# Exponential chains on VectorE in seven operations instead of eight, and a third tile in the fifth chunk of six batches

## The chip, the cores and the metric

The kernel runs on one core of a Trainium2 chip. The metric is the device time of one execution in microseconds (us). Engines are named as in the profile: PE (TensorE, matrix products), DVE (VectorE), ACT (ScalarE), POOL (GpSimd) and SP (SyncE, which here only issues DMAs).

## The reference

The program is soft-capped attention followed by a soft mixture of experts with 8 experts and 32 slots. Inputs are q, k, v of 8 batches x 12 heads x 448 positions x 64.

```python
scores = scale * np.matmul(q, k.transpose(0, 1, 3, 2))     # scale = 1/8
scores = cap * np.tanh(scores / cap)                       # cap = 30
attn = np.exp(scores - np.max(scores, axis=-1, keepdims=True))
attn = attn / (np.sum(attn, axis=-1, keepdims=True) + 1e-09)
x = np.matmul(attn, v)                                     # then (B*S, H*D) = (3584, 768)
logits = x @ phi
slot_input = softmax(logits, axis=0).T @ x                 # 32 slots
slot_out[e] = np.maximum(slot_input[e] @ w1[e], 0) @ w2[e] # 8 experts of 4 slots
out = softmax(logits, axis=1) @ slot_out
```

The two softmaxes of the last part are written out in the original. What the change touches is the exponential of the capped scores; the kernel takes no maximum away, since scores stay within 30.

## The kernel before

Attention is worked off in tiles. Two heads make a pair, two pairs a quad (Q); each pair has seven tiles of scores, a tile being 128 partitions (64 keys of each of the two heads) by 448 queries. The 48 pairs give 336 tiles. Six tiles make a chunk, so there are 56 chunks, seven to a batch of the input. A chunk is worked in two halves of three tiles.

For each half, PE forms the scores (`qk_chunk`, L320) in one of two PSUM tiles `sc`, and ACT writes tanh of them as float16 into the chunk's tile `ex` (`tanh_chunk`, L329). A PSUM tile is free for the scores two halves on when its tanh is done. Then the exponential is taken in place, float16 to bfloat16. ACT does most tiles (`exp_chunk`, `exp_part`, L334); the first tiles of some chunks are done on DVE by a chain of eight elementwise steps (`poly_exp`, L564 to L572) which builds the bits of the bfloat16 number: the first step scales into 16-bit fixed point, the next takes the fraction (`xf`), the next four form a cubic polynomial of it (`xp`), the seventh adds it and the last scales to the bfloat16 pattern. `SHARED` says how many tiles of a chunk go this way, and `POLY` in which place of DVE's queue each step of each chain is issued. All chains use one `xf` and one `xp`.

PE multiplies the exponentials with the values (`pv_first`, `pv_rest`, L590; block-diagonal values `vbd`, cast by POOL at L287) in one PSUM bank `pv`. DVE normalizes (`norm`: reciprocal L597, product L600) into `xq`. Transposes of q and k (`transp`: PE L277 into `qps`/`kps`, DVE copy L279), of the attention output (`x_transp`: PE L638 and L643 into `xps`, DVE copy L652 to `xT`), the logits, the slot sums (`slacc`, L741) and the transposed slot weights all share one PSUM bank with the tag T: each of them waits until the one before has been copied out.

The order on every engine is written by hand. The loop over chunks j has slots; `at(j, slot, f)` hangs work into a slot, and `run(j, slot)` issues what hangs under "<slot", "slot" and ">slot" in that order:

```python
        run(j, "e")          # after the tanh of both halves of chunk j
        exp_chunk(j - 1)     # from j = 3 on
        pv_first(pr); run(j, "a"); pv_tail(pr, 0, CA)
        qk_chunk(2 * j + 2); run(j, "b")
        pv_rest(pr, aux.pop((j, "r"), ())); vcast_after(pr); run(j, "c")
        qk_chunk(2 * j + 3); run(j, "d")
```

The x transpose of a batch's first quad is in slot "a" of the batch's sixth chunk, and q of the next batch's first quad is transposed in slot "b" of the same chunk. Dummy products (`fill` L620, `spare` L835 and L838) keep PE at work. After the last chunk the expert layers and the output follow; they are not touched.

Of the kernel before, what the change touches and what calls it, by code (L numbers as in the profile page):

```python
# [12 lines left out]
U16 = mybir.dt.uint16  # L13
F16 = mybir.dt.float16
ALU = mybir.AluOpType
# [17 lines left out]
STEP = 512  # L33
POW2 = (0.07802411, 0.2260679, 0.69583317, 0.99992526)
# [3 lines left out]
def kernel(  # L38
# [297 lines left out]
    def exp_chunk(j):  # L336
# [4 lines left out]
    SHARED = {1: (2, 0), 3: (2, 0), 4: (3, 0), 6: (1, 0), 7: (3, 0), 9: (3, 0), 11: (2, 0), 12: (3, 0),  # L341
# [4 lines left out]
    POLY = {(1, 'e'): ((1, 0),),  # L346
            (1, '>b'): ((1, 1), (1, 2)),
            (1, 'r'): ((1, 3),),
            (1, '<c'): ((1, 4),),
            (1, '>c'): ((1, 5),),  # L350
            (2, '>a'): ((1, 6),),
            (2, '>c'): ((1, 7),),
            (3, 'e'): ((3, 0), (3, 1), (3, 2)),
            (3, '>b'): ((3, 3),),
            (4, '>a'): ((3, 4), (3, 5), (3, 6), (4, 0)),
            (4, '<c'): ((4, 1),),
            (5, 'e'): ((3, 7), (4, 2)),
            (5, '>a'): ((4, 3),),
            (6, 'e'): ((4, 4), (4, 5)),
            (6, '>a'): ((6, 0), (4, 6), (6, 1)),  # L360
            (6, '>b'): ((6, 2),),
            (6, 'r'): ((4, 7),),
            (6, '<c'): ((6, 3),),
            (6, '>c'): ((6, 4),),
            (6, '>d'): ((6, 5), (6, 6)),
            (7, 'e'): ((7, 0), (6, 7)),
            (7, '>b'): ((7, 1),),
            (7, '>c'): ((7, 2),),
            (7, '>d'): ((7, 3),),
            (8, 'e'): ((7, 4),),  # L370
            (8, '>a'): ((7, 5),),
            (8, '>c'): ((7, 6),),
            (9, '>a'): ((9, 0), (7, 7)),
            (9, '>b'): ((9, 1),),
            (9, '<c'): ((9, 2),),
            (10, 'e'): ((9, 3),),
            (10, '>a'): ((9, 4),),
            (10, '>b'): ((9, 5),),
            (10, '>c'): ((9, 6),),
            (11, 'e'): ((11, 0), (9, 7), (11, 1)),  # L380
            (11, '>a'): ((11, 2),),
            (11, '<c'): ((11, 3),),
            (11, '>d'): ((11, 4), (11, 5), (11, 6)),
            (12, '>a'): ((11, 7), (12, 0)),
            (12, '>b'): ((12, 1),),
            (12, '<c'): ((12, 2),),
            (12, '>c'): ((12, 3),),
            (13, '>b'): ((12, 4),),
            (13, '>c'): ((12, 5),),
            (13, '>d'): ((12, 6),),  # L390
            (14, 'e'): ((14, 0), (12, 7)),
            (14, '>b'): ((14, 1),),
            (14, '>c'): ((14, 2), (14, 3)),
            (14, '>d'): ((14, 4),),
            (15, '>b'): ((14, 5),),
            (15, '>c'): ((14, 6),),
            (15, '>d'): ((14, 7),),
            (16, '>a'): ((16, 0),),
            (16, '>b'): ((16, 1),),
            (16, '>c'): ((16, 2),),  # L400
            (16, '>d'): ((16, 3),),
            (17, 'e'): ((16, 4),),
            (17, '>a'): ((16, 5),),
            (17, '>d'): ((16, 6),),
            (18, 'e'): ((18, 0), (16, 7)),
            (18, '>a'): ((18, 1), (18, 2)),
            (18, '<c'): ((18, 3),),
            (18, '>d'): ((18, 4), (18, 5)),
            (19, 'e'): ((18, 6),),
            (19, '>a'): ((18, 7), (19, 0)),  # L410
            (19, '>b'): ((19, 1),),
            (19, '<c'): ((19, 2),),
            (20, 'e'): ((19, 3),),
            (20, '>b'): ((19, 4), (19, 5)),
            (20, '>d'): ((19, 6),),
            (21, 'e'): ((21, 0), (19, 7)),
            (21, '>b'): ((21, 1),),
            (21, '>c'): ((21, 2), (21, 3)),
            (21, '>d'): ((21, 4),),
            (22, '>b'): ((21, 5),),  # L420
            (22, '>c'): ((21, 6),),
            (22, '>d'): ((21, 7),),
            (23, '>a'): ((23, 0),),
            (23, '>b'): ((23, 1),),
            (23, '>c'): ((23, 2),),
            (23, '>d'): ((23, 3),),
            (24, 'e'): ((23, 4),),
            (24, '>a'): ((23, 5),),
            (24, '>d'): ((23, 6),),
            (25, 'e'): ((25, 0), (23, 7)),  # L430
            (25, '>a'): ((25, 1), (25, 2)),
            (25, '<c'): ((25, 3),),
            (25, '>d'): ((25, 4), (25, 5)),
            (26, 'e'): ((25, 6),),
            (26, '>a'): ((25, 7), (26, 0)),
            (26, '>b'): ((26, 1),),
            (26, '<c'): ((26, 2),),
            (27, 'e'): ((26, 3),),
            (27, '>b'): ((26, 4), (26, 5)),
            (27, '>d'): ((26, 6),),  # L440
            (28, 'e'): ((28, 0), (26, 7)),
            (28, '>b'): ((28, 1),),
            (28, '>c'): ((28, 2), (28, 3)),
            (28, '>d'): ((28, 4),),
            (29, '>b'): ((28, 5),),
            (29, '>c'): ((28, 6),),
            (29, '>d'): ((28, 7),),
            (30, '>a'): ((30, 0),),
            (30, '>b'): ((30, 1),),
            (30, '>c'): ((30, 2),),  # L450
            (30, '>d'): ((30, 3),),
            (31, 'e'): ((30, 4),),
            (31, '>a'): ((30, 5),),
            (31, '>d'): ((30, 6),),
            (32, 'e'): ((32, 0), (30, 7)),
            (32, '>a'): ((32, 1), (32, 2)),
            (32, '<c'): ((32, 3),),
            (32, '>d'): ((32, 4), (32, 5)),
            (33, 'e'): ((32, 6),),
            (33, '>a'): ((32, 7), (33, 0)),  # L460
            (33, '>b'): ((33, 1),),
            (33, '<c'): ((33, 2),),
            (34, 'e'): ((33, 3),),
            (34, '>b'): ((33, 4), (33, 5)),
            (34, '>d'): ((33, 6),),
            (35, 'e'): ((35, 0), (33, 7)),
            (35, '>b'): ((35, 1),),
            (35, '>c'): ((35, 2), (35, 3)),
            (35, '>d'): ((35, 4),),
            (36, '>b'): ((35, 5),),  # L470
            (36, '>c'): ((35, 6),),
            (36, '>d'): ((35, 7),),
            (37, '>a'): ((37, 0),),
            (37, '>b'): ((37, 1),),
            (37, '>c'): ((37, 2),),
            (37, '>d'): ((37, 3),),
            (38, 'e'): ((37, 4),),
            (38, '>a'): ((37, 5),),
            (38, '>d'): ((37, 6),),
            (39, 'e'): ((39, 0), (37, 7)),  # L480
            (39, '>a'): ((39, 1), (39, 2)),
            (39, '<c'): ((39, 3),),
            (39, '>d'): ((39, 4), (39, 5)),
            (40, 'e'): ((39, 6),),
            (40, '>a'): ((39, 7), (40, 0)),
            (40, '>b'): ((40, 1),),
            (40, '<c'): ((40, 2),),
            (41, 'e'): ((40, 3),),
            (41, '>b'): ((40, 4), (40, 5)),
            (41, '>d'): ((40, 6),),  # L490
            (42, 'e'): ((42, 0), (40, 7)),
            (42, '>b'): ((42, 1),),
            (42, '>c'): ((42, 2), (42, 3)),
            (42, '>d'): ((42, 4),),
            (43, '>b'): ((42, 5),),
            (43, '>c'): ((42, 6),),
            (43, '>d'): ((42, 7),),
            (44, '>a'): ((44, 0),),
            (44, '>b'): ((44, 1),),
            (44, '>c'): ((44, 2),),  # L500
            (44, '>d'): ((44, 3),),
            (45, 'e'): ((44, 4),),
            (45, '>a'): ((44, 5),),
            (45, '>d'): ((44, 6),),
            (46, 'e'): ((46, 0), (44, 7)),
            (46, '>a'): ((46, 1), (46, 2)),
            (46, '<c'): ((46, 3),),
            (46, '>d'): ((46, 4), (46, 5)),
            (47, 'e'): ((46, 6), (47, 0)),
            (47, '>a'): ((46, 7), (47, 1)),  # L510
            (47, '>b'): ((47, 2),),
            (47, '<c'): ((47, 3),),
            (47, '>c'): ((47, 4),),
            (48, 'e'): ((48, 0),),
            (48, '>a'): ((47, 5),),
            (48, 'r'): ((47, 6), (47, 7)),
            (48, '>c'): ((48, 1),),
            (48, '>d'): ((48, 2),),
            (49, '>a'): ((48, 3), (48, 4), (49, 0)),
            (49, '<c'): ((48, 5), (48, 6)),  # L520
            (49, '>c'): ((49, 1),),
            (49, '>d'): ((49, 2), (49, 3)),
            (50, '>b'): ((49, 4),),
            (50, '>c'): ((48, 7), (49, 5)),
            (50, '>d'): ((49, 6),),
            (51, 'e'): ((51, 0), (51, 1)),
            (51, '>a'): ((49, 7), (51, 2)),
            (51, '<c'): ((51, 3),),
            (51, '>d'): ((51, 4), (51, 5)),
            (52, 'e'): ((52, 0),),  # L530
            (52, '>a'): ((51, 6),),
            (52, '>b'): ((52, 1),),
            (52, '<c'): ((52, 2), (51, 7)),
            (52, '>d'): ((52, 3),),
            (53, 'e'): ((52, 4), (52, 5)),
            (53, '>a'): ((53, 0), (52, 6)),
# [654 lines left out]
```

## Time and profile before

| what | value |
| --- | --- |
| time, median of 3 runs | 287.41 us (286.95, 287.41, 288.18) |
| span of the profiled execution, first to last instruction | 285.1 us |
| time of the profiled execution with what lies around the span | not listed apart; the median lies 2.3 us above the span |
| busy: PE, DVE, ACT, POOL | 249.9, 243.6, 254.5, 139.4 us |
| mean granted PE clock | 0.983 |
| instructions of the chains on DVE | 34 chains of 8 |
| tiles on DVE | 82 (18 chains of three, 12 of two, 4 of one) |
| ACT exponentials | 21 of six tiles, 4 of five, 12 of four, 19 of three, and some smaller ones |

In the timelines the columns are start and duration in us, engine, line and operation, tiles and shapes, the count, and in brackets the idle time of the engine before it with what ended it. Operations that stand next to each other and are alike are merged in one row. Busy PE is modelled, since products are pipelined. Waits are put down to whatever came last.

The attention part lasts until about 241 us of the span; in it a batch of seven chunks recurs about every 28.8 us.

### The profile page before, as it was taken

How to read it: one execution, taken by the hardware profiler on the slowest of the kernel's cores; microseconds unless marked ns; L12 is line 12 of the kernel's file. 1: busy time of each engine (PE TensorE's matmuls, PEld its weight loads, DVE VectorE, ACT ScalarE, POOL GpSimd, SP SyncE). 2: the span in 40 equal slices, each digit the busy share in tenths (PEclk: the TensorE clock that was granted, in tenths of full speed). 3: DMA queues.
4: the chain of work that ended last, by engine and by line, in shares of the span. 5: the costliest groups of instructions: out<-in, count | busy, mean ns of one | idle time of the engine just before them, and what ended most of it. 6: DMA issues, size and time to landing. Idle time of an engine off the chain costs nothing.

```text
span 285.1 us, 10742 instructions
## 1 busy us (share of the span) xinstructions
PE 249.9 (88%) x4692; PEld 169.8 (60%) x4692; DVE 243.6 (85%) x507; ACT 254.5 (89%) x211; POOL 139.4 (49%) x197
## 2 busy tenths in 40 slices
PE   8888889998999889989998999899899999998720
PEld 7555466756675667566656676667666668552410
DVE  3498999999999999999999999999999986457840
ACT  4999999999999999999999999999999998237730
POOL 7892645664755565565556646564572220200000
PEclk9999999999999999999999999999999999999985
DMA  7999999999999999999999999999999576989997
GB/s 253 241 199 204 216 191 221 217 207 214 218 228 202 205 230 222 228 198 228 226 220 206 218 228 215 209 228 220 223 175 221 129 258 201 409 320 390 410 426 305
DMA packets 58334, 68.10 MB, mean 239 GB/s; under 512 B 4145, under 2 KB 54449, under 8 KB 58289
## 3 DMA queue, kind: packets, MB, share of 16 engines
q0 software_dynamic: 42448, 35.31, 79.4%
q1 hardware_dynamic: 15552, 31.89, 31.9%
q8 instruction: 36, 0.59, 0.8%
q10 hardware_dynamic: 288, 0.23, 0.2%
q14 instruction: 10, 0.07, 0.1%
HBM read 91.72 MB, written 19.27 MB: 389 GB/s over the span
## 4 chain that ended last, share of the span: by engine, by line
DVE 43%; PE 30%; issue 10%; ACT 6%; POOL 6%; DMA 1%; DVEq 0%; ACTq 0%; SPq 0%
PE pv L590 9%; DVE xq L600 7%; PE sc L320 5%; DVE ex L571 4%; DVE xp L570 4%; DVE xT L652 4%; DVE xp L568 3%; POOL vbd L287 3%; DVE qT L279 3%; DVE ex L564 2%; ACT ex L334 2%; DVE xf L566 2%; PE junk L835 2%; DVE xp L569 2%; PE so_ps L1055 2%
## 5 line engine op out<-in xcount | busy, mean ns | idle before, releaser
L329 ACT ACTIVATE ex<-sc 128x1344 f16<-128x1344 f32 (+1 forms) x113 | 149.8, 1454 | 1.4 <-PE sc L320 1.4
L334 ACT ACTIVATE ex<-ex 128x2688 bf16<-128x2688 f16 (+5 forms) x58 | 116.8, 2027 | 0.1
L590 PE MATMUL pv<-vbd,ex 128*128 128x130 bf16 (+1 forms) x1610 | 95.2, 211 | 11.3 <-POOL vbd L287 8.4
L590 PEld LDWEIGHTS <-ex 128*128 128x128 bf16 (+1 forms) x1680 | 75.7, 101 | 36.0 <-PE sc L320 8.9
L320 PE MATMUL sc<-qT,kT 64*64 64x448 bf16 x672 | 71.5, 360 | 0.6 <-DVE qT L279 0.4
L287 POOL CAST vbd<-vraw 64x896 bf16<-64x896 f32 x46 | 46.3, 1006 | 48.9 <-issue 23.9
L600 DVE TENSOR_TENSOR xq<-pv,rec 128x448 bf16<-128x448 f32 x46 | 28.7, 624 | 1.6
L320 PEld LDWEIGHTS <-kT 64*64 64x64 bf16 x672 | 24.2, 105 | 6.4 <-issue 4.2
L295 POOL MEMSET vbd<- 64x1 bf16 x22 | 3.6, 165 | 45.2 <-PE pv L590 45.2
L570 DVE TENSOR_TENSOR xp<-xp,xf 128x1344 f16<-128x1344 f16 (+2 forms) x34 | 25.1, 737 | 0.8
L571 DVE TENSOR_TENSOR ex<-ex,xp 128x1344 uint16<-128x1344 uint16 (+2 forms) x34 | 25.2, 741 | 0.4
L568 DVE TENSOR_TENSOR xp<-xp,xf 128x1344 f16<-128x1344 f16 (+2 forms) x34 | 24.9, 734 | 0.6
L116 POOL DMA_DIRECT2D w1b<-in_moe_w_dram x32 | 25.3, 793 | 0.0
L567 DVE TENSOR_SCALAR xp<-xf 128x1344 f16<-128x1344 uint16 (+2 forms) x34 | 17.0, 501 | 0.4
L184 POOL DMA_DIRECT2D qb<-in_q_dram x22 | 16.7, 758 | 0.8 <-DMA kraw<-in_k_dram 0.8
L279 DVE COPY kT<-kps 128x896 bf16<-128x896 bf16 x23 | 14.1, 615 | 3.1 <-PE kps L274 2.8
L572 DVE TENSOR_SCALAR ex<-ex 128x1344 uint16<-128x1344 uint16 (+2 forms) x34 | 16.4, 484 | 0.1
L277 PEld LDWEIGHTS <-qb 128*64 128x64 bf16 x308 | 10.1, 109 | 10.8 <-issue 10.8
L184 POOL DMA_DIRECT2D kb<-in_k_dram x22 | 16.2, 734 | 0.0
L120 POOL DMA_DIRECT2D w2d<-in_moe_w_dram x21 | 15.9, 777 | 0.4 <-issue 0.4
L620 PE MATMUL pv<-ones 128*128 128x57 bf16 x369 | 15.8, 188 | 0.0
L652 DVE COPY xT<-xps 128x896 bf16<-128x896 bf16 (+1 forms) x24 | 14.3, 597 | 1.7 <-PE xps L643 1.7
(124 smaller groups left out, 343.0 us busy)
## 6 DMA issues: line engine op xcount, KB each, us to landing
w1b<-in_moe_w_dram POOLq DMA_DIRECT2D x32, 384.0 KB, 8.8
vraw<-in_v_dram SPq DMA_DIRECT2D x44, 224.0 KB, 6.1
w2d<-in_moe_w_dram POOLq DMA_DIRECT2D x21, 384.0 KB, 8.4
w2t<-w2d SPq DMA_DIRECT2D x21, 384.0 KB, 7.0
out_dram<-ob SPq DMA_DIRECT2D x7, 768.0 KB, 7.0
qb<-in_q_dram POOLq DMA_DIRECT2D x22, 224.0 KB, 7.4
kb<-in_k_dram POOLq DMA_DIRECT2D x22, 224.0 KB, 6.1
w2b<-in_moe_w_dram POOLq DMA_DIRECT2D x11, 384.0 KB, 8.6
```

Of the source, the lines that this page charges most:

```text
L116: pool.dma_start(out=w1b[e][:, js, fs], in_=w1r[:, e, js, fs])
L184: pool.dma_start(out=t, in_=quad_ap(nm, Q))
L287: pool.tensor_copy(vbds[Q % 2][r, :, :, c0:c0 + DH], raw[r])
L320: pe.matmul(sc[cs, u, 0:S], qkT["k", Q][r, c, cs], qkT["q", Q][r, :, cs], start=True, stop=True)
L329: act.activation(exs[j][:, half * CS + u0:half * CS + u1, :].bitcast(F16), (own[0] if i == u0 == 0 else sc)[:, u0:u1, 0:S], ACT.Tanh, scal ...
L334: act.activation(exs[j][:, u0:u1, :], exs[j][:, u0:u1, :].bitcast(F16), ACT.Exp, scale=cap)
L568: lambda: dve.tensor_tensor(p, p, f, op=ALU.mult),
L570: lambda: dve.tensor_tensor(p, p, f, op=ALU.mult),
L571: lambda: dve.tensor_tensor(y, y, p, op=ALU.add),
L590: pe.matmul(out_, exs[j][r, u, q0:q0 + (HP if tail else P)], v_, start=(c == 0 and g == gs[0] < NF), stop=(c == NT - 1), skip_group_check= ...
L600: dve.tensor_tensor(xq[Q][:, h, s0:s1, :], pv[:, 0:s1 - s0, 0:DH], rec.to_broadcast([P, s1 - s0, DH]), op=ALU.mult)
L652: copy(xTs[Q][:, hs[0]:hs[-1] + 1, :], ps[:, hs[0]:hs[-1] + 1, :])
```

## The change

A chain on DVE has seven steps instead of eight. The fraction is taken with an OR of 512 added in the same instruction, so that it stands for 1 + fraction; its square is formed by one product of the 16-bit integers with the same bits read as float16; one scale-and-add and one product make the polynomial. The fitted constant is moved from the first step to the last.

In chunks 11, 18, 25, 32, 39 and 46, the fifth of their batches, DVE takes three tiles instead of two, so that ACT's exponential of these chunks covers three instead of four. DVE has 88 tiles in all.

`POLY` is written anew: one step fewer for each chain, the others for the most part in the slots where they were. Chunk 39 stands for the six, and its neighbours 37 and 40 for the other chains:

```diff
-POW2 = (0.07802411, 0.2260679, 0.69583317, 0.99992526)
+POW2 = (0.45804578, 0.46570838, 0.07629315)
...
-    SHARED = {... 37: (3, 0), 39: (2, 0), 40: (3, 0), ...}
+    SHARED = {... 37: (3, 0), 39: (3, 0), 40: (3, 0), ...}
...
             (37, '>a'): ((37, 0),),
             (37, '>b'): ((37, 1),),
-            (37, '>c'): ((37, 2),),
-            (37, '>d'): ((37, 3),),
-            (38, 'e'): ((37, 4),),
-            (38, '>a'): ((37, 5),),
-            (38, '>d'): ((37, 6),),
-            (39, 'e'): ((39, 0), (37, 7)),
-            (39, '>a'): ((39, 1), (39, 2)),
-            (39, '<c'): ((39, 3),),
-            (39, '>d'): ((39, 4), (39, 5)),
-            (40, 'e'): ((39, 6),),
-            (40, '>a'): ((39, 7), (40, 0)),
+            (37, '>d'): ((37, 2),),
+            (38, 'e'): ((37, 3),),
+            (38, '>a'): ((37, 4),),
+            (38, '>d'): ((37, 5),),
+            (39, 'e'): ((39, 0), (37, 6)),
+            (39, '>a'): ((39, 1),),
+            (39, '<c'): ((39, 2),),
+            (39, '>d'): ((39, 3), (39, 4)),
+            (40, 'e'): ((39, 5),),
+            (40, '>a'): ((39, 6), (40, 0)),
             (40, '>b'): ((40, 1),),
-            (40, '<c'): ((40, 2),),
-            (41, 'e'): ((40, 3),),
-            (41, '>b'): ((40, 4), (40, 5)),
-            (41, '>d'): ((40, 6),),
+            (41, 'e'): ((40, 2),),
+            (41, '>b'): ((40, 3), (40, 4)),
+            (41, '>d'): ((40, 5),),
...
-    c3, c2, c1, c0 = (c * STEP ** (1 - n) for c, n in zip(POW2, (3, 2, 1, 0)))
-    c1, c0 = c1 - 1, c0 - STEP
+    c0, c1, c3 = POW2
...
-        y, f, p = t.bitcast(U16), xf[x][:, 0:n1], xp[x][:, 0:n1]
+        y, s, p = t.bitcast(U16), xf[x][:, 0:n1], xp[x][:, 0:n1]
         steps = (
-            lambda: dve.tensor_scalar(y, t.bitcast(F16), octaves * STEP, base * STEP + c0,
+            lambda: dve.tensor_scalar(y, t.bitcast(F16), octaves * STEP, base * STEP,
                                       ALU.mult, ALU.add),
-            lambda: dve.tensor_scalar(f, y, STEP - 1, None, ALU.bitwise_and),
-            lambda: dve.tensor_scalar(p, f, c3, c2, ALU.mult, ALU.add),
-            lambda: dve.tensor_tensor(p, p, f, op=ALU.mult),
-            lambda: dve.tensor_scalar(p, p, c1, None, ALU.add),
-            lambda: dve.tensor_tensor(p, p, f, op=ALU.mult),
+            lambda: dve.tensor_scalar(s, y, STEP - 1, STEP, ALU.bitwise_and, ALU.bitwise_or),
+            lambda: dve.tensor_tensor(p, s, s.bitcast(F16), op=ALU.mult),
+            lambda: dve.tensor_scalar(p, p, c3 * 2 ** 24 / STEP ** 2, c1 - 1, ALU.mult, ALU.add),
+            lambda: dve.tensor_tensor(p, p, s, op=ALU.mult),
             lambda: dve.tensor_tensor(y, y, p, op=ALU.add),
-            lambda: dve.tensor_scalar(y, y, 128.0 / STEP, 128.0 * (127 - base),
+            lambda: dve.tensor_scalar(y, y, 128.0 / STEP, 128.0 * (127 - base + c0),
                                       ALU.mult, ALU.add))
```

More of the change, by code (lines that the diff above doesn't have):

```diff
@@ new lines @@
+            (1, '>b'): ((1, 1),),
+            (1, 'r'): ((1, 2),),
+            (1, '<c'): ((1, 3),),
+            (1, '>c'): ((1, 4),),
+            (2, '>a'): ((1, 5),),
+            (2, '>c'): ((1, 6),),
+            (3, 'e'): ((3, 0), (3, 1)),
+            (3, '>b'): ((3, 2),),
+            (4, '>a'): ((3, 3), (3, 4), (3, 5), (4, 0)),
+            (4, '<c'): ((4, 1),),
+            (5, 'e'): ((3, 6),),
+            (5, '>a'): ((4, 2),),
+            (6, 'e'): ((4, 3), (4, 4)),
+            (6, '>a'): ((6, 0), (4, 5), (6, 1)),
@@ new lines @@
+            (6, 'r'): ((4, 6),),
+            (6, '<c'): ((6, 2),),
+            (6, '>c'): ((6, 3),),
+            (6, '>d'): ((6, 4), (6, 5)),
+            (7, 'e'): ((7, 0), (6, 6)),
+            (7, '>b'): ((7, 1),),
+            (7, '>d'): ((7, 2),),
+            (8, 'e'): ((7, 3),),
+            (8, '>a'): ((7, 4),),
+            (8, '>c'): ((7, 5),),
+            (9, '>a'): ((9, 0), (7, 6)),
+            (9, '>b'): ((9, 1),),
+            (10, 'e'): ((9, 2),),
+            (10, '>a'): ((9, 3),),
@@ new lines @@
+            (10, '>b'): ((9, 4),),
+            (10, '>c'): ((9, 5),),
+            (11, 'e'): ((11, 0), (9, 6), (11, 1)),
+            (11, '<c'): ((11, 2),),
+            (11, '>d'): ((11, 3), (11, 4), (11, 5)),
+            (12, '>a'): ((11, 6), (12, 0)),
+            (12, '>b'): ((12, 1),),
+            (12, '>c'): ((12, 2),),
+            (13, '>b'): ((12, 3),),
+            (13, '>c'): ((12, 4),),
+            (13, '>d'): ((12, 5),),
+            (14, 'e'): ((14, 0), (12, 6)),
+            (14, '>b'): ((14, 1),),
@@ L398 @@
+            (14, '>c'): ((14, 2),),
+            (14, '>d'): ((14, 3),),
+            (15, '>b'): ((14, 4),),
+            (15, '>c'): ((14, 5),),
+            (15, '>d'): ((14, 6),),
             (16, '>a'): ((16, 0),),
             (16, '>b'): ((16, 1),),
[L400 to L406, printed above, removed]
@@ L420 @@
-            (22, '>b'): ((21, 5),),
-            (22, '>c'): ((21, 6),),
-            (22, '>d'): ((21, 7),),
+            (16, '>d'): ((16, 2),),
+            (17, 'e'): ((16, 3),),
+            (17, '>a'): ((16, 4),),
+            (17, '>d'): ((16, 5),),
+            (18, 'e'): ((18, 0), (16, 6)),
+            (18, '>a'): ((18, 1),),
+            (18, '<c'): ((18, 2),),
+            (18, '>d'): ((18, 3), (18, 4)),
+            (19, 'e'): ((18, 5),),
+            (19, '>a'): ((18, 6), (19, 0)),
@@ L423 @@
+            (19, '>b'): ((19, 1),),
+            (20, 'e'): ((19, 2),),
+            (20, '>b'): ((19, 3), (19, 4)),
+            (20, '>d'): ((19, 5),),
+            (21, 'e'): ((21, 0), (19, 6)),
+            (21, '>b'): ((21, 1),),
+            (21, '>c'): ((21, 2),),
+            (21, '>d'): ((21, 3),),
+            (22, '>b'): ((21, 4),),
+            (22, '>c'): ((21, 5),),
+            (22, '>d'): ((21, 6),),
             (23, '>a'): ((23, 0),),
             (23, '>b'): ((23, 1),),
-            (23, '>c'): ((23, 2),),
@@ L439 @@
-            (27, '>b'): ((26, 4), (26, 5)),
-            (27, '>d'): ((26, 6),),
-            (28, 'e'): ((28, 0), (26, 7)),
-            (28, '>b'): ((28, 1),),
[L443 to L447, printed above, removed]
+            (23, '>d'): ((23, 2),),
+            (24, 'e'): ((23, 3),),
+            (24, '>a'): ((23, 4),),
+            (24, '>d'): ((23, 5),),
@@ new lines @@
+            (25, 'e'): ((25, 0), (23, 6)),
+            (25, '>a'): ((25, 1),),
+            (25, '<c'): ((25, 2),),
+            (25, '>d'): ((25, 3), (25, 4)),
+            (26, 'e'): ((25, 5),),
+            (26, '>a'): ((25, 6), (26, 0)),
+            (26, '>b'): ((26, 1),),
+            (27, 'e'): ((26, 2),),
+            (27, '>b'): ((26, 3), (26, 4)),
+            (27, '>d'): ((26, 5),),
+            (28, 'e'): ((28, 0), (26, 6)),
+            (28, '>b'): ((28, 1),),
+            (28, '>c'): ((28, 2),),
@@ L448 @@
+            (28, '>d'): ((28, 3),),
+            (29, '>b'): ((28, 4),),
+            (29, '>c'): ((28, 5),),
+            (29, '>d'): ((28, 6),),
             (30, '>a'): ((30, 0),),
             (30, '>b'): ((30, 1),),
[L450 to L457, printed above, removed]
@@ L471 @@
-            (36, '>c'): ((35, 6),),
-            (36, '>d'): ((35, 7),),
+            (30, '>d'): ((30, 2),),
+            (31, 'e'): ((30, 3),),
+            (31, '>a'): ((30, 4),),
+            (31, '>d'): ((30, 5),),
+            (32, 'e'): ((32, 0), (30, 6)),
+            (32, '>a'): ((32, 1),),
+            (32, '<c'): ((32, 2),),
+            (32, '>d'): ((32, 3), (32, 4)),
+            (33, 'e'): ((32, 5),),
+            (33, '>a'): ((32, 6), (33, 0)),
+            (33, '>b'): ((33, 1),),
@@ L473 @@
+            (34, 'e'): ((33, 2),),
+            (34, '>b'): ((33, 3), (33, 4)),
+            (34, '>d'): ((33, 5),),
+            (35, 'e'): ((35, 0), (33, 6)),
+            (35, '>b'): ((35, 1),),
+            (35, '>c'): ((35, 2),),
+            (35, '>d'): ((35, 3),),
+            (36, '>b'): ((35, 4),),
+            (36, '>c'): ((35, 5),),
+            (36, '>d'): ((35, 6),),
             (37, '>a'): ((37, 0),),
             (37, '>b'): ((37, 1),),
-            (37, '>c'): ((37, 2),),
-            (37, '>d'): ((37, 3),),
@@ L498 @@
+            (43, '>b'): ((42, 4),),
+            (43, '>c'): ((42, 5),),
+            (43, '>d'): ((42, 6),),
             (44, '>a'): ((44, 0),),
             (44, '>b'): ((44, 1),),
[L500 to L513, printed above, removed]
+            (44, '>d'): ((44, 2),),
+            (45, 'e'): ((44, 3),),
+            (45, '>a'): ((44, 4),),
+            (45, '>d'): ((44, 5),),
+            (46, 'e'): ((46, 0), (44, 6)),
+            (46, '>a'): ((46, 1),),
+            (46, '<c'): ((46, 2),),
+            (46, '>d'): ((46, 3), (46, 4)),
@@ L514 @@
+            (47, 'e'): ((46, 5), (47, 0)),
+            (47, '>a'): ((46, 6), (47, 1)),
+            (47, '<c'): ((47, 2),),
+            (47, '>c'): ((47, 3),),
             (48, 'e'): ((48, 0),),
-            (48, '>a'): ((47, 5),),
-            (48, 'r'): ((47, 6), (47, 7)),
+            (48, '>a'): ((47, 4),),
+            (48, 'r'): ((47, 5), (47, 6)),
             (48, '>c'): ((48, 1),),
-            (48, '>d'): ((48, 2),),
-            (49, '>a'): ((48, 3), (48, 4), (49, 0)),
-            (49, '<c'): ((48, 5), (48, 6)),
+            (49, '>a'): ((48, 2), (48, 3), (49, 0)),
@@ L521 @@
+            (49, '<c'): ((48, 4), (48, 5)),
             (49, '>c'): ((49, 1),),
[L522 to L525, printed above, removed]
+            (49, '>d'): ((49, 2),),
+            (50, '>b'): ((49, 3),),
+            (50, '>c'): ((48, 6), (49, 4)),
+            (50, '>d'): ((49, 5),),
             (51, 'e'): ((51, 0), (51, 1)),
-            (51, '>a'): ((49, 7), (51, 2)),
-            (51, '<c'): ((51, 3),),
@@ L538 @@
-            (53, '<c'): ((53, 2), (53, 3)),
-            (54, 'e'): ((53, 4),),
-            (54, '>b'): ((53, 5), (53, 6)),
+            (52, '<c'): ((51, 6),),
+            (52, '>d'): ((52, 2),),
+            (53, 'e'): ((52, 3), (52, 4)),
+            (53, '>a'): ((53, 0), (52, 5)),
+            (53, '>b'): ((52, 6), (53, 1)),
+            (53, '<c'): ((53, 2),),
+            (54, 'e'): ((53, 3),),
+            (54, '>b'): ((53, 4), (53, 5)),
             (54, '<c'): ((54, 0),),
-            (54, '>c'): ((53, 7), (54, 1), (54, 2), (54, 3)),
```

107 lines of the change are left out of this document (11 added, 96 removed), and 6 rows, old and new, of the table SHARED.

## The prediction

> **What bounds the kernel now.** I read the page's first part, then the busy times in stretches of one batch, then the timelines of ACT, DVE and PE over one batch, and last the list of waits.
>
> ```profile
> PE 249.9 (88%) x4692; PEld 169.8 (60%) x4692; DVE 243.6 (85%) x507; ACT 254.5 (89%) x211; POOL 139.4 (49%) x197
> ```
> ```profile
> 151.10:179.80 28.70, 26.72 (x553) 18.80 (x551) 27.93 (x57) 28.70 (x23) 17.40 (x25) 1.00 1.25 218
> ```
> The second is one batch; its columns are length, then PE, weight loads, DVE, ACT, POOL busy, then clock, DMA share and GB/s. ACT is busy for all of it, DVE for 97%, PE for 93%, at a full granted clock. The timeline of ACT says the same:
>
> ```profile
> 31.76 1.29 ACT L329 ACTIVATE ex<-sc 128x1344 f16<-128x1344 f32 x1 [0.34 <-PE sc L320]
> 140.47 2.63 ACT L334 ACTIVATE ex<-ex 128x2688 bf16<-128x2688 f16 x1
> 169.24 2.76 ACT L334 ACTIVATE ex<-ex 128x2688 bf16<-128x2688 f16 x1
> ...
> 173.91 2.04 ACT L334 ACTIVATE ex<-ex 128x1792 bf16<-128x1792 f16 x1
> 175.50 2.81 ACT L329 ACTIVATE ex<-sc 128x1344 f16<-128x1344 f32 x2
> ```
> The same exponential of three batches ends at 143.10, 172.00 and, with a start of 198.00 and 2.90, at 200.90: 28.90 apart both times. So ACT sets the pace. But durations of one shape creep up while starts run ahead, so a start is not when work began, and ACT's spare time must be read from ends. Where a tanh truly waited for PE (31.76, ending 33.05), its scores had ended at 31.72 (PE's L320 from 31.15, 0.57): end of scores to end of tanh takes at least 1.33. The spare time of any tanh is that distance less 1.33.
>
> The tightest place comes once a batch: the second tanh of the pair at 175.50, ending 178.31, in the seventh stage. Its scores are the last line here (PE, then DVE ahead of it):
>
> ```profile
> 173.67 0.25 PE L643 MATMUL xps<-ident,xq 64*64 64x64 bf16 x4
> ...
> 174.74 0.58 PE L277 MATMUL qps<-ident,qb 128*64 128x128 bf16 x14 [0.32 <-DVE xT L652]
> 175.25 0.90 PE L590 MATMUL pv<-vbd,ex 128*128 128x130 bf16 x15
> 176.04 0.57 PE L320 MATMUL sc<-qT,kT 64*64 64x448 bf16 x6
> ```
> ```profile
> 170.78 0.21 DVE L597 RECIPROCAL rec<-pv 128x7 f32<-128x7 f32 x1
> 171.02 0.62 DVE L600 TENSOR_TENSOR xq<-pv,rec 128x448 bf16<-128x448 f32 x1
> 171.56 0.68 DVE L568 TENSOR_TENSOR xp<-xp,xf 128x896 f16<-128x896 f16 x1
> 172.16 0.38 DVE L741 TENSOR_TENSOR slacc<-slps,slacc 128x224 f32<-128x224 f32 x1
> 172.46 0.38 DVE L569 TENSOR_SCALAR xp<-xp 128x896 f16<-128x896 f16 x1
> 172.87 0.62 DVE L570 TENSOR_TENSOR xp<-xp,xf 128x896 f16<-128x896 f16 x1
> 173.53 0.62 DVE L571 TENSOR_TENSOR ex<-ex,xp 128x896 uint16<-128x896 uint16 x1
> 174.07 0.61 DVE L652 COPY xT<-xps 128x896 bf16<-128x896 bf16 x1
> ```
> The spare time there is 178.31 - 176.60 - 1.33 = 0.38. Read likewise (0.01 apart by rounding) it is 0.05, 0.40, 0.09, 0.24, 0.37 and 0.13 in the six batches, 1.28 in sum. DVE is why: after the norm (L600) it runs four steps of the fifth chunk's chain, here the two-tile one, and only then copies xT. PE has turned xps by 173.92, the copy starts at 174.07, and PE's qps waits for it because both use the one psT bank. The sixth batch shows what more steps do:
>
> ```profile
> 202.91 0.39 DVE L564 TENSOR_SCALAR ex<-ex 128x896 uint16<-128x896 f16 x1
> 203.21 0.62 DVE L652 COPY xT<-xps 128x896 bf16<-128x896 bf16 x1
> ```
> ```profile
> 203.88 0.58 PE L277 MATMUL qps<-ident,qb 128*64 128x128 bf16 x14 [0.64 <-DVE xT L652]
> ```
>
> **The change, part by part.** *ACT.* In six batches the fifth chunk's exponential covers three tiles instead of four: rows 173.91 to 175.50 (1.59) against 177.84 to 179.05 (1.21), 0.38 each, 2.3 us in all. This is the whole possible gain, as ACT has no other work less.
>
> *DVE's total.* By the groups kept apart by shape, a three-tile chain costs 534+501+610+854+506+855+864+579 = 5303 ns, a two-tile one 4041. The new chain drops one TENSOR_SCALAR (L567, 610). Its and/or step is nearest to L566 (501), its s*s to L568 (854, which already mixes f16 with 16-bit integers), the next to L569 (506): 5303-610 = 4693. A batch goes from 3x5303+4041 = 19950 to 4x4693 = 18772 ns, 1.18 less, so DVE as a total is no bound. The two new kinds are not in the trace. From below I take the shortest three-tile row, 0.50; from above the slope of the f32 rows L741 (224 elements, 381 ns) and L600 (448, 624), which gives 1.60 for 1344 elements. I take the near rows, same size and type width; the upper end is a rival.
>
> *Order on DVE, on the path.* What counts is start to start. With three tiles a TENSOR_TENSOR takes 0.77 to a next step that doesn't need it (150.69 to the copy at 151.47) and 0.89 to one that does (155.86 to 156.76); a TENSOR_SCALAR 0.42 and 0.53 (150.16 to 150.69). Between norm and xT copy the new program issues s*s, slacc, scale-and-add, product and sum of three tiles. Norm to copy was 0.54+0.60+0.30+0.41+0.66+0.54 = 3.05; it becomes 0.54+0.77+0.30+0.53+0.89+0.77 = 3.80. The dropped step lies ahead of the norm, whose start waits for PE, so it gives nothing here. The copy comes 0.75 later, and with it qps, the 15 pv products and the scores, since PE's queue is in order. The trace has this experiment in small: the sixth batch has one more step (L564, 0.30) ahead of the copy, and qps waits 0.64 instead of 0.32.
>
> [...]
>
> *Returned on DVE.* The step dropped at '<c' of the third stage (163.25, 0.42) lies ahead of the qT copy, so DVE reaches the fourth stage's reciprocal (166.81, behind L570) 0.42 sooner. PE's wait of 0.15 before the pv at 167.73, for DVE xq L600, goes; what is late next is PE's own lps. Net on the path: 0.75 - 0.15 = 0.60 a batch. After the copy one more three-tile step stands before the next norm, about 0.13 on PE's junk wait.
>
> *Sum.* Per batch the tanh is late by 0.60 less its spare time: 6 x 0.60 - 1.28 = 2.3 us. The 0.38 that ACT saves lies ahead of this tanh and is spent waiting there. It isn't won back: PE's scores two halves on wait for ACT's tanh (they start 0.05 to 0.2 after its end: 164.86 after 164.75), so the next batch begins as late. If instead PE alone sets the pace afterwards, spare time counts less and the 0.13 is added: 6 x 0.73 = 4.4 less 0 to 1.28, so up to 4. The first batch and the tail keep their tile counts; their dropped steps lie beside ACT, which runs without a gap until 240.95, and I cost them at nothing (0.3 either way were that cover gone). PE, POOL and the queues issue the same instructions. The profiled span is 285.1; the three times have the median 287.41, 2.3 more, which I carry over: 285.1 + 2.3 + 2.3 = 289.7.
>
> **Rivals.** *ACT's saving comes through* (faster): the place has room after all, if the new steps pass quicker than their rows or PE is freed earlier. It decides if norm to copy stays below about 3.2. Then 287.4 - 2.3 = 285.1. For it: ACT is busy without a gap, DVE's total falls. Against it: four operations of three tiles stand ahead of the copy and each has its row.
>
> *It cancels* (within 0.5%, 1.4 us, about what a measurement can tell from no change): the lateness is half of what I add, as where PE regains time at its POOL waits (0.88 at 155.56): 287.4 + 0.5 = 287.9.
>
> *A new form runs slow*: s*s at the f32 slope costs 0.75 more, again between norm and copy: per batch 0.38 + 0.75 = 1.13, so 294.2. [...]
>
> That the change doesn't do what it says I exclude: the guard on base + octaves (45 + 43.3) is far below 127.
>
> **How the numbers follow.** My case 0.69 (of it 0.09 within 0.5%), saving comes through 0.17 (0.01 within), cancelling 0.08, slow form 0.06. Slower 0.60+0.06 = 0.66, same 0.18, faster 0.16. The likeliest case alone gives 288.2 to 291.6. The range reaches down to the saving's 285.1 and up to 291.8, leaving out the slow form and little else.
>
> **What would show it.** Right: L652 starts about 3.8 after the norm in the fifth chunk's batches; qps waits about 1 us for xT L652; ACT shows waits for PE sc L320, one a batch, and its ends lie 29.1 to 29.5 apart; DVE's busy time falls by some 9. Wrong: the ends lie 28.5 apart, or norm to copy is near 3.1, or a step of three tiles takes over 1 us.

## The result, and the profile after

The changed kernel takes 293.78 us (median of four runs, 290.39 to 295.09) where the kernel before takes 287.55 in the same four rounds (286.95 to 288.18). The ratio is 1.0137, with a 95% interval of [1.0095, 1.0179]; the two runs with the lowest granted PE clock are left out of it. It is slower. The profiled execution took 295.09 us with a span of 293.3, and its mean clock was 0.965.

The page of the changed kernel, its first part and the row of the granted clock over 40 equal slices:

```profile
PE 254.9 (87%) x4692; PEld 172.1 (59%) x4692; DVE 238.6 (81%) x473; ACT 253.9 (87%) x211; POOL 139.9 (48%) x197
...
PEclk9999999999999999999978999999969999999995
```

DVE has 34 instructions fewer and is busy for 5.0 us less, ACT for 0.6 less, POOL for 0.5 more, and the span is 8.2 longer. PE's 5.0 more go with the two dips of the clock row (in e2, with as many products and no dip, PE is busy for 250.1, 0.2 more than before). Busy times in three neighbouring stretches (length, then PE, weight loads, DVE, ACT, POOL, clock, DMA share, GB/s) show both losses apart:

```profile
120.20:149.70 29.50, 26.41 (x543) 18.56 (x537) 27.83 (x52) 28.64 (x22) 17.16 (x25) 1.00 1.25 217
149.70:157.00 7.30, 7.30 (x84) 3.75 (x79) 5.38 (x10) 6.25 (x5) 4.55 (x6) 0.53 1.14 182
157.00:179.50 22.50, 20.76 (x450) 15.14 (x447) 20.07 (x40) 21.49 (x17) 13.25 (x18) 1.00 1.15 195
```

In the first stretch, at full clock, ACT is idle for 0.86 of 29.50, where it was busy for the whole of the batch shown of the kernel before. In the second PE runs at half clock and is busy without a gap. The list of waits (total, times, longest) names the first loss (the changed kernel's, then that of the kernel before):

```profile
ACT ex L329 <- PE sc L320: 9.1, 12, 1.5
...
PE qps L277 <- DVE xT L634: 8.8, 7, 1.9
```
```profile
PE qps L277 <- DVE xT L652: 2.5, 7, 0.6
ACT ex L329 <- PE sc L320: 1.4, 2, 1.1
```

The timeline of DVE in the third batch shows why (start, duration; L582 is the norm, L550 the square, L634 the xT copy):

```profile
114.10 0.62 DVE L582 TENSOR_TENSOR xq<-pv,rec 128x448 bf16<-128x448 f32 x1
114.64 0.92 DVE L550 TENSOR_TENSOR xp<-xf 128x1344 f16<-128x1344 uint16 x1
115.48 0.38 DVE L723 TENSOR_TENSOR slacc<-slps,slacc 128x224 f32<-128x224 f32 x1
115.78 0.49 DVE L551 TENSOR_SCALAR xp<-xp 128x1344 f16<-128x1344 f16 x1
116.31 0.86 DVE L552 TENSOR_TENSOR xp<-xp,xf 128x1344 f16<-128x1344 f16 x1
117.20 0.86 DVE L553 TENSOR_TENSOR ex<-ex,xp 128x1344 uint16<-128x1344 uint16 x1
117.98 0.61 DVE L634 COPY xT<-xps 128x896 bf16<-128x896 bf16 x1
```

Norm to copy is 3.88, 0.82 more than before. PE and ACT follow:

```profile
118.64 0.58 PE L277 MATMUL qps<-ident,qb 128*64 128x128 bf16 x14 [1.25 <-DVE xT L634]
119.16 0.90 PE L572 MATMUL pv<-vbd,ex 128*128 128x130 bf16 x15
120.01 0.57 PE L320 MATMUL sc<-qT,kT 64*64 64x448 bf16 x6
```
```profile
120.62 1.29 ACT L329 ACTIVATE ex<-sc 128x1344 f16<-128x1344 f32 x1 [0.61 <-PE sc L320]
```

Read in this way for the six batches: norm to copy 3.88, 4.56, 3.88, 4.21, 3.88, 4.53; ACT's wait 0.57, 1.13, 0.61, 1.28, 1.16, 1.51; no tanh at this place has any spare time left: each ends 1.33 after its scores, the least that the prediction reckoned with. The whole 8.2 is there when the last tanh ends (238.45 before, 246.64 after).

### The profile page after: what moved, and what is told of

Its sections match the earlier page's. It is cut to its first block, busy times and chain, and to the rows that moved or that the text cites. A ratio compares the mean times of both kernels' runs of the same rounds, so it can differ in the third digit from the quotient of the medians.

```text
span 293.3 us, 10708 instructions
## 1 busy us (share of the span) xinstructions
PE 254.9 (87%) x4692; PEld 172.1 (59%) x4692; DVE 238.6 (81%) x473; ACT 253.9 (87%) x211; POOL 139.9 (48%) x197
## 4 chain that ended last, share of the span: by engine, by line
PE 39%; ACT 21%; DVE 21%; issue 9%; POOL 5%; DMA 1%; DVEq 0%; SPq 0%; ACTq 0%
PE pv L572 13%; ACT ex L329 12%; ACT ex L334 7%; PE sc L320 6%; DVE xq L582 3%; POOL vbd L287 3%; DVE ex L553 2%; DVE xp L550 2%; DVE xp L552 2%; PE so_ps L1037 2%; PE hp L1009 2%; DVE xT L634 2%; PE junk L817 2%; PE kps L277 1%; DVE xp L551 1%
## 5 line engine op out<-in xcount | busy, mean ns | idle before, releaser
L329 ACT ACTIVATE ex<-sc 128x1344 f16<-128x1344 f32 (+1 forms) x113 | 142.5, 1311 | 9.2 <-PE sc L320 9.1
L334 ACT ACTIVATE ex<-ex 128x1344 bf16<-128x1344 f16 (+5 forms) x58 | 106.1, 1832 | 0.1
L320 PE MATMUL sc<-qT,kT 64*64 64x448 bf16 x672 | 73.0, 370 | 0.8 <-DVE qT L279 0.4
L287 POOL CAST vbd<-vraw 64x896 bf16<-64x896 f32 x46 | 44.3, 964 | 54.2 <-issue 29.1
L582 DVE TENSOR_TENSOR xq<-pv,rec 128x448 bf16<-128x448 f32 x46 | 28.7, 624 | 1.6
L550 DVE TENSOR_TENSOR xp<-xf 128x1344 f16<-128x1344 uint16 (+2 forms) x34 | 28.0, 824 | 0.1
L552 DVE TENSOR_TENSOR xp<-xp,xf 128x1344 f16<-128x1344 f16 (+2 forms) x34 | 26.5, 779 | 0.8
L277 PE MATMUL qps<-ident,qb 128*64 128x128 bf16 x308 | 12.8, 222 | 9.0 <-DVE xT L634 8.8
L547 DVE TENSOR_SCALAR ex<-ex 128x1344 uint16<-128x1344 f16 (+2 forms) x34 | 17.0, 500 | 1.4 <-ACT ex L329 1.3
L551 DVE TENSOR_SCALAR xp<-xp 128x1344 f16<-128x1344 f16 (+2 forms) x34 | 17.3, 509 | 0.6
L279 DVE COPY qT<-qps 128x896 bf16<-128x896 bf16 x23 | 14.2, 619 | 3.6 <-PE qps L277 3.2
```

Of the source, the lines that this page charges most:

```text
L277: pe.transpose(ps[h * HP:h * HP + HP, c, :], src[:, h, c * DH:(c + 1) * DH], ident)
L279: dve.tensor_copy(t, ps)
L287: pool.tensor_copy(vbds[Q % 2][r, :, :, c0:c0 + DH], raw[r])
L320: pe.matmul(sc[cs, u, 0:S], qkT["k", Q][r, c, cs], qkT["q", Q][r, :, cs], start=True, stop=True)
L329: act.activation(exs[j][:, half * CS + u0:half * CS + u1, :].bitcast(F16), (own[0] if i == u0 == 0 else sc)[:, u0:u1, 0:S], ACT.Tanh, scal ...
L334: act.activation(exs[j][:, u0:u1, :], exs[j][:, u0:u1, :].bitcast(F16), ACT.Exp, scale=cap)
```

## Experiments

Time is the median of the runs; the ratio is to runs of the kernel before on the same chip (287.48 for e1 to e4, 287.09 for e5 to e7, 287.34 for e8 and e9).

**e1: the new chain, two tiles.** Chunks 11, 18, 25, 32, 39 and 46 alike:

```diff
-    SHARED = {... 39: (3, 0), ...}
+    SHARED = {... 39: (2, 0), ...}
```

> The seven-step chains alone: the fifth chunk of the six batches keeps two tiles on VectorE, every step stays in its new place. Path theory (the copy of xT is late because four steps of three tiles stand ahead of it): norm to copy of xT is back at 0.54+0.60+0.30+0.41+0.66+0.54 = 3.05 us, ScalarE waits for scores only as often as before the change, its exponentials end 28.9 us apart, the clock stays near 0.983, and the time is that of before, 286.9 to 288.0 us. Rival (the seven-step operations themselves are what costs, the new product of one tile read in two types above all): norm to copy stays near 3.9 and the time near 290 us or above.

Measured 286.78 us, 0.1 under the range expected, ratio 0.998 [0.9963, 0.9996]. Norm to copy is 3.06 five times and 3.36, as before, and ACT waits nowhere between 32 and 241 us. So with two tiles neither the new operations nor the new order on DVE cost anything. Groups of this kernel kept apart by shape (mean ns of one) price the new ones at two tiles:

```profile
L550 DVE TENSOR_TENSOR xp<-xf 128x896 f16<-128x896 uint16 x12 | 8.0, 666 | 0.1
...
L549 DVE TENSOR_SCALAR xf<-ex 128x896 uint16<-128x896 uint16 x12 | 4.9, 410 | 0.1
```

The nearest product of before, L568, had 669 at this size: no slow form.

**e2: the old chain, three tiles.** The kernel before, with `39: (3, 0)` in place of `(2, 0)` in the six chunks.

> The third tile alone, with the chains of eight steps and their places of before. Path theory: norm to copy is 0.54+0.77+0.30+0.53+0.89+0.77 = 3.80 us, so it is as slow as the changed kernel, 290 to 293 us; VectorE has 19.95 - 4.04 + 5.30 = 21.2 us of chains a batch, over 29 us in all with its other work, so a further 0.3 to 0.6 us a batch is possible (up to 296). Rival (the new operations cost): 285 to 288 us, as ScalarE has one tile less.

Measured 293.22 us, ratio 1.02 [1.0177, 1.0224], at a clock never below 0.983. Norm to copy is 3.81 to 4.41 (3.80 expected). The third tile alone makes the loss, and with the longer chains a larger one; its waits:

```profile
ACT ex L329 <- PE sc L320: 9.2, 8, 1.6
...
PE qps L277 <- DVE xT L652: 7.4, 7, 1.5
```

**e3: the changed kernel, with the sum step moved behind the copy.** Chunks 18, 25 and 32 as 39 here; 11 and 46 likewise, with their neighbours a little different:

```diff
-            (40, 'e'): ((39, 5),),
-            (40, '>a'): ((39, 6), (40, 0)),
-            (40, '>b'): ((40, 1),),
+            (40, '>a'): ((39, 5),),
+            (40, '>b'): ((39, 6), (40, 0)),
+            (40, '<c'): ((40, 1),),
```

> The changed kernel with only the order on VectorE altered in the six batches: the fifth chunk's sum step is issued behind the copy of xT, its last step and the next chain's first two behind the copy of qT. Path theory: norm to copy falls to 0.54+0.85+0.30+0.53+0.77 = 2.99 us, the wait of qps to 0.3, ScalarE waits no more and its exponentials end 28.5 us apart: 285 to 286 us, faster than both. Rival (ScalarE's saving can't come through, because TensorE with VectorE and GpSimd is as long as ScalarE): the waits go but the ends stay 28.8 to 28.9 apart, 287 to 288 us. A second rival (the total work on VectorE or a new operation is what costs): no better than 290.

Measured 285.71 us, ratio 0.9926 [0.9906, 0.9945]. All the work of the change is there; only the order differs. The timeline of DVE in the same batch:

```profile
114.97 0.86 DVE L553 TENSOR_TENSOR xp<-xp,xf 128x1344 f16<-128x1344 f16 x1
115.75 0.62 DVE L635 COPY xT<-xps 128x896 bf16<-128x896 bf16 x1
116.28 0.85 DVE L554 TENSOR_TENSOR ex<-ex,xp 128x1344 uint16<-128x1344 uint16 x1
```

Norm to copy is 2.98 or 2.99 in three batches and 3.32 to 3.47 in the others, and ACT waits at this tanh only in the third, fourth and sixth batch (0.15, 0.07 and 0.52). The gain of 1.8 to 2.1 us in the median is near the 2.3 that ACT saves. The profile shows less of it: the ends of this tanh lie 28.58 to 29.16 apart, not 28.5, and the five batches between the first and the sixth of them are together 0.67 shorter than before. In five of the six no spare time is left, so PE comes just in time here. This version beats both kernels.

**e4: the changed kernel, with PE's wait filled.** Thirty small products behind the x transpose, into the unused `pv` bank:

```diff
+    for c in (11, 18, 25, 32, 39, 46):
+        at(c + 1, "<b", fill, 30)
```

> The changed kernel with 30 dummy products (about 1.0 us) on TensorE in front of the transpose of q that waits for the copy of xT, in the six batches. Theory of two parts (about 0.6 us a batch of lateness, and on top two stretches of 6.8 us at half clock that follow the long idle of TensorE): the lateness stays, the clock stays at 0.983 in all runs, the time is 289.5 to 290.5 us and steady from run to run. Rival (the clock falls for another reason, or by chance in any run): half clock again in some runs, 290 to 295 us, spread as before. Second rival (the dummies delay the products): slower by another 0.1 to 0.5 us a batch.

Measured 291.65 us, above the 289.5 to 290.5 expected, ratio 1.0126 [1.0105, 1.0147], clock 0.981 or more in every run. The fill does not delay qps (the copy's start to qps is 0.67 in both), and the lateness stays: ACT's waits are 0.57, 0.92, 0.58, 1.08, 0.61, 1.20. Page and timeline of PE:

```profile
PEclk9999999999999999999999999999999999999985
```
```profile
145.87 0.97 PE L602 MATMUL pv<-ones 128*128 128x57 bf16 x30
147.43 0.58 PE L277 MATMUL qps<-ident,qb 128*64 128x128 bf16 x14 [0.59 <-DVE xT L634]
```

The half-clock stretch is gone where the wait is filled.

**e5: the changed kernel once more, unchanged,** for the share of the clock.

> The changed kernel as it is, on the same chip as the next two. Two-part theory (lateness at the copy of xT, and half-clock stretches of TensorE that follow the long wait): in some runs the mean granted clock is 0.965 to 0.98 and these are 1 to 4 us longer than the kernel with the filled wait (291.65 us); runs without a half-clock stretch are at 290.4 to 291.8 us. Rival (the filled wait changed nothing, the clock falls by chance of the chip): the clock is 0.982 or above in all runs here too.

Measured 290.41 us (seven runs), ratio 1.0099 [1.007, 1.0128]. Five runs at a clock of 0.981 or more took 289.4 to 290.5; the two at 0.97 and 0.959 took 292.4 and 294.8. The first of these two is profiled:

```profile
PEclk9999999999999999999999999999869999999975
```
```profile
207.08 0.58 PE L277 MATMUL qps<-ident,qb 128*64 128x128 bf16 x14 [2.17 <-DVE xT L634]
207.60 0.90 PE L572 MATMUL pv<-vbd,ex 128*128 128x130 bf16 x15
208.38 0.84 PE L320 MATMUL sc<-qT,kT 64*64 64x448 bf16 x6
209.15 0.68 PE L677 MATMUL eps<-ident,E 128*32 128x128 bf16 x16
209.76 0.50 PE L817 MATMUL junk<-ones 128*128 128x384 bf16 x1
210.20 0.95 PE L320 MATMUL sc<-qT,kT 64*64 64x448 bf16 x6
```

The six scores take 0.57 at full clock and 0.95 here; the records show half clock from 208.5 to 215.4. So lateness alone costs 2.3 to 3.4 us over the 287.09 of before, and the two runs of lower clock took 2.2 and 4.6 more (from 290.25, the middle of the five). The trace of the result shows the price of a dip: its fifth batch takes 31.60 where e4's takes 29.25, and from this tanh in the sixth batch to the last tanh it takes 33.05 where e4 takes 31.23.

The filled kernel holds its clock, but it is no faster: its five runs took 290.4 to 291.8, the five undisturbed ones here 289.4 to 290.5.

**e6 and e7: weight loads put off,** on e3 and on e4, to find why norm to copy is 0.3 or more longer in three of six batches:

```diff
-        at(1 + n * (NCH - 5) // len(wjobs), "b", *job)
+        jw = 1 + n * (NCH - 5) // len(wjobs)
+        at(jw + (jw in (11, 18, 25, 32, 39, 46)), "b", *job)
```

> The kernel with the sum step behind the copy of xT (285.71 us), and GpSimd's issue of one weight load in each of the six fifth stages put off to the next stage. Theory (a TensorScalar of three tiles takes 0.83 instead of 0.50 us while GpSimd issues a weight load, and in every second batch that step is the one ahead of the copy): norm to copy is 2.99 us in all six batches instead of 3.33 in three, ScalarE waits no more in them, 284.7 to 285.4 us. Rival (the stretch has another cause): norm to copy stays at 3.3 in three batches, 285.4 to 286.2 us. Second rival (the stretch moves to the next stage and hits the path there): ScalarE waits elsewhere, 285.5 to 287 us.

> The kernel with the filled wait (291.65 us), with the same weight issues put off by a stage. It sizes the part of the lateness that the prediction left out. Theory: norm to copy is 3.88 us in all batches instead of 4.2 to 4.5 in three, ScalarE waits 0.6 us a batch instead of 0.9 to 1.2 in three: 290.3 to 290.8 us, 1.0 us faster than with the filled wait alone. Rival (the stretch costs nothing on the whole, what PE loses here it gains at GpSimd's waits): 291.3 us or above.

Measured 286.11 us, ratio 0.9964 [0.9946, 0.9983], where 284.7 to 285.4 was expected, and 290.19 us, ratio 1.0099 [1.0076, 1.0122], where it was 290.3 to 290.8. In both the fourth batch is rid of its stretch and the fifth has it instead. My placing was wrong: slot "b" of the next stage comes on POOL right behind the cast that runs beside the norm, so that more loads queue at the place in question. DVE and POOL in the fifth batch of e6:

```profile
170.54 1.50 POOL L120 DMA_DIRECT2D w2d<-in_moe_w_dram  x2
170.81 0.82 DVE L552 TENSOR_SCALAR xp<-xp 128x1344 f16<-128x1344 f16 x1
```

**What stretches.** The changed kernel's timelines of DVE and POOL, second, third and fourth batch:

```profile
84.67 0.92 POOL L287 CAST vbd<-vraw 64x896 bf16<-64x896 f32 x1 [2.51 <-DMA vraw<-in_v_dram]
84.71 1.59 DVE L550 TENSOR_TENSOR xp<-xf 128x1344 f16<-128x1344 uint16 x1
...
115.54 0.99 POOL L120 DMA_DIRECT2D w2d<-in_moe_w_dram  x1
115.78 0.49 DVE L551 TENSOR_SCALAR xp<-xp 128x1344 f16<-128x1344 f16 x1
...
144.90 0.76 POOL L120 DMA_DIRECT2D w2d<-in_moe_w_dram  x1
145.16 0.83 DVE L551 TENSOR_SCALAR xp<-xp 128x1344 f16<-128x1344 f16 x1
```

In the second batch the square starts 0.04 after POOL's cast and takes 0.74 longer than its 0.85. In the other two the same pair of instructions meets, and one of the two is stretched: the load's issue to 0.99 (third) or the TENSOR_SCALAR to 0.83 (fourth), by 0.02 of difference in their starts. I then compared the three-tile steps of nine profiles (before, after, e1 to e7): with no POOL instruction beside it, none of 341 TENSOR_SCALARs took over 0.51. A TENSOR_TENSOR that starts with 0.20, 0.30, 0.36 or 0.67 of a cast still to run takes 0.06, 0.17, 0.22 or 0.54 longer, the rest of the cast less 0.13; one that starts ahead of the cast takes no longer. It goes the other way too: in the changed kernel's profile a cast that starts with 0.22 to 0.39 of a three-tile product still to run takes 1.04 to 1.21, and with 0.10 or 0.08 left 0.95 or 0.96. Weight-load issues do not stretch TENSOR_TENSORs: the 21 of that profile with issues alone beside them, one of them under way at the start, take 0.85 or 0.86, as with nothing beside them. So in these traces a TENSOR_TENSOR and a cast exclude each other, and so do a TENSOR_SCALAR and the issue of a load. With a cast, the one that starts first wins. With the issue of a load the recorded starts do not say it: in all eleven profiles none of the 105 three-tile TENSOR_SCALARs that start up to 0.23 us after the start of an issue is stretched, all of the 109 that start 0.28 to 0.49 after it take 0.59 or more, and in between it is 29 of 100. So the issue holds the step only from about 0.26 us after its recorded start, and the copy at 3.88 or at 4.21 hangs on hundredths of a microsecond.

**e8 and e9: those loads behind POOL's next cast,** on e3 and on e4:

```diff
-        at(1 + n * (NCH - 5) // len(wjobs), "b", *job)
+        jw = 1 + n * (NCH - 5) // len(wjobs)
+        at(jw, "d" if jw in (12, 19, 26, 33, 40, 47) else "b", *job)
```

> The chains' sum step stands behind the xT copy as in e3, and the weight loads that POOL issued in slot "b" of stages 12, 19, 26, 33, 40 and 47 are issued in slot "d" of the same stage, so behind POOL's next cast of vbd, which comes after the copy. Theory: a DVE step and a POOL instruction exclude each other, whichever starts first. A TENSOR_SCALAR of three tiles that starts while POOL issues a weight load is held (0.82 instead of 0.50), a TENSOR_TENSOR that starts while POOL casts vbd is held until 0.13 before the cast's end. Then the TENSOR_SCALAR between norm and copy takes 0.50 in all six batches (e3: 0.83 in the fourth and 0.81 in the sixth), norm to copy is 2.99 in the first, third, fourth and fifth batch, and what is above that in the second and sixth is the square's wait for the cast alone (0.4 at most where the v load lands late); time 285.0 to 285.6 (ratio 0.991 to 0.993; e3 0.9926). Rival (the stretch wanders, as from the fourth batch to the fifth in e6, whatever POOL does there): some TENSOR_SCALAR at this place still takes 0.8, time 286 or more (0.996).

> The changed kernel with PE's wait filled as in e4, and the same weight loads issued behind POOL's next cast. Same theory: the TENSOR_SCALAR between norm and copy takes 0.50 in all six batches (e4: 0.83 in the fourth, 0.81 in the sixth), norm to copy 3.88 in the first, third, fourth and fifth batch and 4.18 in the sixth (one step more), ACT's ends lie 29.2 to 29.3 apart in the fourth and fifth; 0.8 us less than e4, ratio 1.0095 to 1.011. Rival (the stretch comes to other batches): some TENSOR_SCALAR there takes 0.8, ratio as e4's 1.0126 or e7's 1.0099 with a batch at 4.2.

The cause is as expected: the TENSOR_SCALAR takes 0.49 in all six batches of both. ("A DVE step and a POOL instruction exclude each other" is wider than the traces: the issue of a load does not hold a TENSOR_TENSOR, 0.85 or 0.86 with it and without.) Norm to copy in e8 is 2.98 or 2.99 four times, 3.34 in the second batch and 3.17 in the sixth; in e9 it is 3.88 five times and 4.18. DVE in its fourth batch:

```profile
144.03 0.49 DVE L551 TENSOR_SCALAR xp<-xp 128x1344 f16<-128x1344 f16 x1
```

The times are not: 285.99 us, ratio 0.9952 [0.9931, 0.9973], and 290.86 us, ratio 1.0135 [1.0105, 1.0166]. e9's last tanh ends at 240.27, 0.75 sooner than e4's 241.02, but the time from there to the end grew by 0.4. Nor is the 0.75 shown to come from the stretch: e7, which has it in two batches, ends its last tanh at 240.19, and e9's fourth batch is 29.43 long, where 29.2 to 29.3 was expected. In e8 the third and fifth batch became longer (29.53 and 29.13, against 28.79 and 28.60 in e3), ahead of this place. What else the moved loads meet stays open. So these runs show what stretches the step, and not what the stretch costs in all. The best version stays e3.

## Why the prediction came out as it did

**Direction, mechanism, size.** I forecast 289.7, range 285.1 to 291.8. The runs of e5 without a dip of the clock, 289.4 to 290.5, and 1.0137 x 287.4 = 291.3 by the first ratio are in the range; the first median, 293.78, is above it, by the clock. The chain of steps is as forecast: e2 shows that the third tile makes the loss, e3 that it does so by its place ahead of the copy. The size is short: the lateness is more than the 2.3 forecast, and the clock, which the forecast left out, comes on top.

**Norm to copy 3.80.** Measured 3.88 in three batches. The 0.07 is the end of a cast, which holds the square: it takes 0.92 with its next step 0.84 later, not 0.77. In the other three it was 4.21 to 4.56 (the sixth has one step more, 0.30). This term was sized from rows that had no POOL work beside them, and "PE, POOL and the queues issue the same instructions" was the step that failed: the same instructions at POOL met other ones at DVE. With two tiles the TENSOR_SCALAR starts 1.44 after the norm, as POOL's issue does; with three it starts at 1.68, 0.24 or more after the issue, where hundredths decide.

**The 0.15 returned and the spare time.** In batches without a stretched step the two hold on average. The predicted addition is 0.60 less 0.21 of spare time, 0.39 a batch; the filled kernel's third and fifth batch, from end to end of this tanh, are 29.23 and 29.25 long, 0.33 and 0.35 over the 28.90 of before (0.51 and 0.23 by the spare times of these two alone). In the second, fourth and sixth they are 29.56, 29.72 and 29.84.

**The sum.** Predicted +2.3. Profiles have to be compared from a common place, since even the same kernel starts differently: the first norm is at 22.75 in the result's profile and at 21.89 in e5's (22.87 before, 21.96 in e4, 22.07 in e7 and e9). From the first norm to the last tanh's end it takes 215.58 before. In e4, without dips of the clock, it takes 3.5 more; in e9, without the stretched TENSOR_SCALARs, 2.6; in e7, with two of them, 2.5. So the lateness was forecast about 1 us too small. Norm to copy, longer than 3.80 by 1.6 in the sum of e4's six batches (the sixth's extra step left out), is large enough for that; as e7, where it is 1.4, loses no more than e9, where it is 0.5, how much of it reaches the end stays open.

From the last tanh to the end it takes 48.1 to 48.6 in e4, e7 and e9, but 46.7 to 47.0 in the profiles of before, after and e5. That is the fill's own price. The lines of the DMAs (instruction loads; output writes, with the median time from issue to landing), before and in e4:

```profile
q8 instruction: 36, 0.59, 0.8%
...
out_dram<-obh SPq DMA_DIRECT2D x14, 192.0 KB, 2.0
```
```profile
q8 instruction: 38, 0.62, 0.8%
...
out_dram<-obh SPq DMA_DIRECT2D x14, 192.0 KB, 3.6
```

The 180 added products make PE's program longer (4872 products for 4692). The three filled profiles are the only ones with 38 instruction loads, and the only ones with one about 21 us after the last tanh; five output writes issued from 18.9 to 21.5 us after it land 3.9 to 4.5 us later, where 2.0 to 2.8 is usual. That the load holds the writes is not tested. So the filled kernels' times do not measure lateness alone.

**Signs.** qps waits 1.15 to 1.88 (about 1 forecast). ACT's waits are there, one a batch. The ends lie 29.25 to 31.60 apart, mostly above the 29.1 to 29.5 forecast, and 29.2 to 29.8 where no dip of the clock adds to them (e4). DVE's busy time fell by 5.0, not by some 9: a square of three tiles averages 0.94, not 0.854, and the steps stretched by POOL count as busy. One sign of being wrong did appear: steps of three tiles took over 1 us, the square at this place 1.59 and the next chunk's 1.07 (120.47 in POOL's timeline is a cast, 121.07 in DVE's the square). It is the meeting with the cast and not the form: squares with nothing of POOL beside them take 0.85.

**Rivals.** "Saving comes through" was decided by the limit I gave, norm to copy below about 3.2; it is e3 that meets it, in three of its six batches. "A new form runs slow" falls with e1 (666 ns for the new square, 669 for the nearest product of before); its small chance was my estimate, as no run had shown such a product. "It cancels" falls with the ratio's interval. The rival that I had not named is the clock. Its dips follow some of the waits that the change made longer, and they carry the first median past my range.

## What to carry to other kernels

Before work is added on an engine with time to spare, look for what stands next in its queue for another engine: the same work behind the xT copy gained 0.7%, ahead of it it lost 1%. Where DVE and GpSimd both work at a place, price a step on DVE by the rows that had GpSimd beside them (here 0.83 instead of 0.49 for a TENSOR_SCALAR, 1.59 instead of 0.85 for a square), and ask what the step's new start will meet. Waits on PE of 1.50, 1.88 and 2.17 us were followed here by 6.8 us at half clock, four others of 1.49 to 1.56 were not: a wait that grows may cost more than itself. Removing it paid here (e3); filling it held the clock but cost as much elsewhere, 291.65 us against 290.41 unfilled.

## What the hardware showed that was not expected

In the 20 us before the two dips of the changed kernel's profile PE was busy for 90% and 88%. There and in e5 a wait for the copy of 1.50, 1.88 or 2.17 us was followed, 1.4 to 1.6 us after its end, by 6.8 us at half clock. It is no certain consequence: waits of 1.56 in the same profile, of 1.55 and 1.49 in e5's and of 1.52 in e2's had none, and five of e5's seven runs have the mean clock of runs without one. As 1.50 was followed by a dip and 1.56 was not, no limit for the wait comes out of this. Of the eleven runs without the fill (the result's and e5's) five have a mean clock of 0.975 or less. In the 17 runs of e4, e7 and e9, where the fill leaves 1.0 or less of the wait, the clock was never under 0.978.

In these traces GpSimd's issue of a load holds a three-tile TENSOR_SCALAR of DVE by up to some 0.33 us (0.83 for 0.50), but only one that starts 0.24 us or more after it; it is itself held, from 0.76 to 0.99, by one that starts 0.24 after it.
